# Batch 0's q side head by head, with its k-by-v sum turned by VectorE, and a new issue order batch by batch

## The chip, the cores and the metric

The kernel runs on one core of a Trainium2 chip. The metric is the device time of one execution in microseconds (us). TensorE is PE, VectorE DVE, ScalarE ACT, GpSimd POOL, and SyncE SP, which issues the transfers.

## The reference

```python
def phi(x):                       # x: [4 batches, 4 heads, 1088, 32]
    a = einsum('rd,bhsd->bhsr', S1, x); b = einsum('rd,bhsd->bhsr', S2, x)   # r = 8
    return einsum('bhsi,bhsj->bhsij', a, b).reshape(*x.shape[:-1], 64)
q_p, k_p = phi(q), phi(k)
kv = einsum('bhsf,bhsd->bhfd', k_p, v);  z = sum(k_p, axis=2)
attn = einsum('bhsf,bhfd->bhsd', q_p, kv) / (einsum('bhsf,bhf->bhs', q_p, z)[..., None] + 1e-06)
x = attn.transpose(0, 2, 1, 3).reshape(4352, 128)
h = x @ w_in                      # 128 -> 2048
out = (h - tanh(h)) @ w_out       # 2048 -> 128
```

The inputs and the output are float32; the two large products run in bfloat16.

## The kernel before

The work has two parts. **Attention** makes `xT`, the 4352 normalised rows turned to 128 partitions (4 heads of 32) by 4352 columns, batch by batch, 1088 columns each. The **FFN** takes `xT` in ten column groups (`GCOLS`), of 256, 384, 448, six of 512, and 192 columns. For each group `ffn` runs 16 matmuls `h` (one for each 128 rows of the hidden layer), 16 tanh `th` on ACT, 16 matmuls `o` with `w_out`, and two more `o` with `wch` and `wcl`, the product w_in·w_out in two bfloat16 halves, which stand for the linear part h @ w_out. The sum lies in PSUM bank 3; VectorE transposes it (`ot`) and SP stores it (`st`). The `h` results use PSUM banks 0 to 2, attention banks 4 to 7.

For each batch the **k side** transposes k (`kT`, VectorE), multiplies it by the small S1/S2 matrix (`ksk`, PE), transposes back (`kab`, VectorE), forms the 64 products of each row (`w`, three pieces of 768 columns, VectorE or POOL) and sums them with v (`kvmm`, three pieces of 24 matmuls on PE). `gram`, `gm`, `scmm` and `sc` get the weights of the denominator. `kv_tail` then turns the 128x64 sum into the stationary operand of the numerators: ACT or VectorE copies it out of PSUM four times side by side (`kvd`), PE transposes it (`kvt`), and it is copied out again (`kvb`).

The **q side** transposes q (`qT`), sketches it (`qsk`, PE, 16 tiles of 32x32, into four banks), transposes back (`abc`), makes the denominator and divides (`m`, `den`, `rd`, `aq`), forms the products (`qp`, pieces of 512 or 768 columns), transposes them (`qpT`) and multiplies by kv (`num`, PE, 32 matmuls of all 16 tiles, four banks). Two copies (`x`) put the result into `xT`. Batch 0's q side is cut into blocks 0 to 2 (256 columns) and 2 to 9, the latter with numerators for 2 to 5 and 5 to 9.

The names carry the batch and piece: `kT2.0.0` is batch 2's first k transpose, `h1.0` group 1's first matmul, `o1.3` its fourth of the second layer, `lk1.0` the first half of batch 1's k load. `wi` and `wo` are casts of the weights to bfloat16, `wit`/`wiT` a transpose of w_in on PE and its copy out by ACT, `wc` the product w_in·w_out on PE; all `wc` wait for the last `wo` cast.

Every engine issues its instructions in an order written out in `TABLE`: a token is an operation's number, the letter of its engine, and its buffer; `f` and `F` are filler matmuls on zeros, 256 and 512 columns long. `plan` reads it, and `sync` adds the waits. An engine that waits holds back all that is queued behind it. A load also waits until the loads ahead of it leave at most `CAP` bytes in flight:

```python
if o.big:
    left = CAP - o.dma[0]
    for p in reversed(loads):
        left -= p.dma[0]
        if left < 0:
            o.deps.setdefault(p, False)
```

The orders around the change, before:

```
PE   ksk0 6F gram0 f F scmm0 kvmm0.0 qsk0.0 kvmm0.1 F F wit0 wit1 kvmm0.2 wit2 kvt0 F F num0.0 wit3 qsk0.2 | h0.. o0.. wc.. num0.2 wc3 num0.5
     h1.0 h1.1 o0.11 ksk1 o0.12 h1.2 .. ksk2 .. kvmm1, gram1, kvmm2, kvmm3, kvt1-3 among h1, o1 | h2.. qsk1.0 qsk2.0 .. num1.0 h3.0-2 num1.5 .. qsk3.0 .. num2.0 in h4 .. num3.0 in h5
DVE  kT0 .. kab0.0 qT0.0 kab0.1 w0.0-2 abc0.0 den rd qpT0.0 qT0.1 abc0.2 m den rd qp0.2 qpT0.2 qpT0.5 qpT0.7 kT1.0.0 kT1.1.0 kT2.0.0 wcl kab1.0 kab1.1 x0.5.1 kT2.1.0 ot0 ..
ACT  gm0 sc0 wi0 wi1 wi2 kvd0 wo0 kvb0 wiT0 x0.0.0 x0.0.1 wiT1 th0.0 ..
POOL m0.0 aq0.0 qp0.0 wi3 wo1 wo2 wo3 aq0.2 qp0.5 qp0.7 w1.0 w1.1 w1.2 w2.0 w2.1 m1.0 qp1.. 
SP   lk0.0 sin1 lk0.1 lq0 lv0 lwi0-3 lwo0 lq0.1 lwo1-3 lk1 lq1 lv1 lk2 lq2 lv2 lk3.0 st0.0 lk3.1 lq3 ..
```

## Time and profile before

| | |
|---|---|
| Time, median of 3 runs | 112.78 us (111.4, 112.78, 112.95) |
| The profiled execution's own time | 111.28 us |
| Its span, first to last instruction | 109.1 us |
| Granted TensorE clock | 0.999 of full speed, the 2.4 GHz level |
| Busy PE / ACT / DVE / POOL | 97.9 / 80.8 / 58.4 / 30.3 us |
| HBM read / written | 8.95 / 2.23 MB |

Busy time of PE counts from the start of a matmul to its modelled end, and matmuls overlap, so a busy PE can still be waiting a little. A row of the timeline gives start, duration, engine, line, operation, output and input; in brackets stands the idle time ahead of it and what ended that. Lines of the code: L349 all copies, L438 loads, L528 `kT`, L540 `qT`, L548 `ksk`, L589 `w`, L604 `kvmm`, L622 `kvt`, L643 `qsk`, L686 `qp`, L702 `num`, L802 `h`, L806 `th`, L817 `o`, L826 `ot`.

### The profile page before, as it was taken

The numbers are of one execution on the slowest core, as the hardware profiler recorded it, in microseconds if no ns is written. First come the engines' busy times: TensorE is split into PE (matmuls) and PEld (weight loads), VectorE is DVE, ScalarE is ACT, GpSimd is POOL, SyncE is SP. The second block draws the span as 40 slices with busy tenths as digits, with TensorE's granted clock in tenths as the row PEclk, the third lists the DMA queues.
The fourth block names the chain that finished last, engine by engine and source line by source line (L and its number), as shares of the span: only waits on it lengthen the run. The fifth ranks groups of instructions, "written<-read, shape, count | busy, mean of one in ns | idle before, by whom it ended". The sixth has DMA issues, their size and how long they took to land.

```text
span 109.1 us, 3403 instructions
## 1 busy us (share of the span) xinstructions
PE 97.9 (90%) x1460; PEld 47.9 (44%) x1467; DVE 58.4 (54%) x91; ACT 80.8 (74%) x166; POOL 30.3 (28%) x48
## 2 busy tenths in 40 slices
...
GB/s 84 219 232 280 220 254 300 266 248 302 261 153 320 215 13 3 6 72 0 6 25 56 9 26 71 6 0 96 0 0 12 90 1 53 43 0 28 71 62 70
DMA packets 25918, 11.38 MB, mean 104 GB/s; under 512 B 19120, under 2 KB 23600, under 8 KB 25904
## 3 DMA queue, kind: packets, MB, share of 16 engines
...
q10 hardware_dynamic: 560, 0.07, 0.4%
...
HBM read 8.95 MB, written 2.23 MB: 102 GB/s over the span
## 4 chain that ended last, share of the span: by engine, by line
PE 54%; DMA 20%; DVE 10%; SPq 7%; POOL 3%; issue 2%
PE psb L817 22%; PE psb L802 20%; DMA wo_f<-in_moe_w_out_dram 8%; DMA kL<-in_k_dram 8%; SPq L438 7%; PE psb L702 5%; DMA wi_f<-in_moe_w_in_dram 5%; DVE kT L528 3%; PE psb L821 2%; POOL qp L686 2%; PE psb L604 2%; DVE w L589 2%; PE psb L643 1%; DVE abk L554 1%; DVE abc L648 1%
## 5 line engine op out<-in xcount | busy, mean ns | idle before, releaser
L806 ACT ACTIVATE th<-psb 128x512 bf16<-128x512 f32 (+4 forms) x136 | 70.1, 618 | 8.3 <-PE psb L802 5.8
L802 PE MATMUL psb<-xT,wi 128*128 128x512 bf16 (+4 forms) x154 | 46.3, 347 | 1.8 <-DVE wcl L788 1.0
L817 PE MATMUL psb<-th,wo 128*128 128x512 bf16 (+4 forms) x160 | 45.4, 348 | 0.4 <-issue 0.3
L802 PEld LDWEIGHTS psb<-xT,wi 128*128 128x128 bf16 x160 | 14.9, 97 | 23.8 <-ACT th L806 11.4
L826 DVE STREAM_TRANSPOSE ot<-psb 128x512 f32<-128x512 f32 (+4 forms) x10 | 6.3, 626 | 31.4 <-PE psb L817 31.4
L817 PEld LDWEIGHTS psb<-th,wo 128*128 128x128 bf16 x160 | 15.2, 98 | 13.2 <-issue 0.8
L686 POOL TENSOR_TENSOR qp<-ap,abc 128x512 f32<-128x512 f32 (+1 forms) x10 | 13.8, 1393 | 5.7 <-DVE ap L668 5.5
L691 DVE STREAM_TRANSPOSE qpT<-qp 128x768 f32<-128x768 f32 (+1 forms) x14 | 11.8, 854 | 2.8 <-POOL qp L686 2.6
L702 PE MATMUL psb<-qpT,kvb 32*32 32x128 f32 (+4 forms) x448 | 8.3, 309 | 1.7 <-ACT kvb L349 1.0
L528 DVE STREAM_TRANSPOSE kT<-kL 128x576 f32<-128x576 f32 (+3 forms) x10 | 5.9, 612 | 6.5 <-DMA kL<-in_k_dram 6.5
L589 POOL TENSOR_TENSOR w<-abk 128x768 f32<-128x768 f32 x5 | 7.5, 1518 | 5.6 <-DVE abk L554 5.6
L413 PE MATMUL psb<-zz 128*128 128x512 bf16 x21 | 7.5, 501 | 0.0
L702 PEld LDWEIGHTS psb<-qpT,kvb 32*32 32x32 f32 x448 | 5.2, 103 | 4.9 <-ACT kvb L349 1.5
L589 DVE TENSOR_TENSOR w<-abk 128x768 f32<-128x768 f32 x7 | 7.2, 1071 | 0.1
L648 DVE STREAM_TRANSPOSE abc<-psb 128x1152 f32<-128x1152 f32 (+2 forms) x5 | 5.7, 1140 | 1.8 <-PE psb L643 1.8
L660 POOL TENSOR_TENSOR m<-abc 128x288 f32<-128x288 f32 (+1 forms) x3 | 2.5, 844 | 14.4 <-DVE abc L648 14.4
L604 PE MATMUL psb<-w,vL 128*32 128x64 f32 x288 | 6.1, 222 | 0.3 <-POOL w L589 0.3
L540 DVE STREAM_TRANSPOSE qT<-qL 128x1088 f32<-128x1088 f32 (+2 forms) x5 | 5.2, 1057 | 0.9 <-DMA qL<-in_q_dram 0.9
L579 ACT COPY gm<-psb 128x32 f32<-128x32 f32 x4 | 0.8, 188 | 6.5 <-PE psb L569 6.5
L604 PEld LDWEIGHTS psb<-w,vL 128*32 128x32 f32 x288 | 4.6, 109 | 1.8 <-issue 0.6
L686 DVE TENSOR_TENSOR qp<-ap,abc 128x768 f32<-128x768 f32 x4 | 4.6, 1157 | 0.7 <-POOL ap L668 0.7
L548 PE MATMUL psb<-kT,wab 64*32 64x288 f32 x64 | 3.3, 472 | 1.7 <-DVE kT L528 0.9
...
## 6 DMA issues: line engine op xcount, KB each, us to landing
...
```

Of the source, the lines that this page charges most:

```text
L413: "F": lambda e, n: e.matmul(bank(3), zz.ap[:, 0:128], zz.ap[:, None, 128:384].to_broadcast([128, 2, 256]), start=True, stop=True)}, zop)
L438: op = P.add({x: 180.0 + 2.1 * rows for x in (eng if isinstance(eng, tuple) else (eng,))}, lambda e, n: e.dma_start(out=o_, in_=i_), w=w, ...
L528: P.add(_v(nb * 32 * (r1 - r0)), lambda e, n, e_=e_, nb=nb, r0=r0, r1=r1: e.transpose(kT[b].ap.rearrange("p (j u t r) -> p r j u t", u=2, ...
L589: P.add({**_v(768), **_gt(768)}, lambda e, n: e.tensor_tensor(out=wv.ap.rearrange("p (x i j) -> p x i j", i=8, j=8), in0=abh(0)[:, :, :, N ...
L604: i = e.matmul(pv[b].ap[h * 32:(h + 1) * 32, 0:64], vL[b][:, h, blk * 32:(blk + 1) * 32], wvs[b, p].ap[:, (bi * 4 + h) * 64:(bi * 4 + h + ...
L648: P.add(_vp(sn * 4), lambda e, n: e.transpose(abc.ap.rearrange("p k h f -> p h k f")[:, :, 0:s1 - s0, :], psa4[:, :, 0:sn].rearrange("p h ...
L686: P.add({**_v(cn * 256), **_gt(cn * 256)}, lambda e, n, qp=qp, c0=c0, cn=cn: e.tensor_tensor(out=qp.ap[:, 0:cn * 256].rearrange("p (x i j) ...
L691: P.add(_v(cn * 256), lambda e, n, qp=qp, o0=o0, cn=cn: e.transpose(qt.ap[:, o0 * 256:(o0 + cn) * 256], qp.ap[:, 0:cn * 256]), r=[qp], w=[ ...
L702: i = e.matmul(psa4[h * 32:(h + 1) * 32, g, 0:nb * 32], kvb.ap[g * 32:(g + 1) * 32, x, h * 32:(h + 1) * 32], qq[g * 32:(g + 1) * 32, 0:nb, ...
L802: P.add(_mm(n_), lambda e, n, jb=jb, hv=hv: e.matmul(hv.ap[:, jb % m * 512:jb % m * 512 + n_], wi[jb // 4].ap[:, (jb % 4) * 128:(jb % 4 + ...
L806: P.add(_a(n_ * m), lambda e, n, hv=hv, th=th: e.activation(out=th.ap.rearrange("p (u x) -> p u x", u=m)[:, :, 0:n_], in_=hv.ap.rearrange( ...
L817: fn = lambda e, n, x=x, st=st, sp_=sp_: e.matmul(ov.ap[:, 0:n_], wo[x // 4].ap[:, x % 4, :], ths[x][0].ap[:, ths[x][1] * 512:ths[x][1] * ...
```

## The change

- Batch 0's q side is cut at blocks of 8, 13 and 13 chunks of 32 columns (`CUT0`), so 256, 416 and 416 columns, and the first groups become 256, 416, 416. Each group of the first three now needs just one piece.
- `kv_heads` replaces `kv_tail(0)`: one VectorE transpose of the 128x64 sum (`kvh`), from PSUM to SBUF. `kvd0`, `kvt0` and `kvb0` go.
- `q_heads` sketches with 4 matmuls and makes numerators with 8, each on the tile of one head (rows and columns h·32), into one bank instead of four, and as long as the piece. Products come in pieces of 512; 448 and 384; 448 and 384 columns.
- Batch 0's remaining q load is cut as its two pieces are. `CAP` is 1.45e6 for 1.3e6. `occ` is a cost for the planner and does nothing on the chip.
- `TABLE` is new. Batch 1's k and q sides are issued ahead of batch 2's, and batch 3's k side moves from group 1 into groups 3 to 6.

```diff
--- before.py
+++ after.py
@@ -16,53 +16,54 @@
 AF = mybir.ActivationFunctionType
 AX = mybir.AxisListType
 
-GCOLS = [256, 384, 448] + [512] * 6 + [192]
-CAP = 1.3e6
+GCOLS = [256, 416, 416] + [512] * 6 + [192]
+CAP = 1.45e6
 PAIRS = 7
-PIECES = {0: [(0, 2), (2, 5), (5, 9)], 1: [(0, 5), (5, 9)], 2: [(0, 9)], 3: [(0, 9)]}
+CUT0 = [0, 8, 21, 34]
+PIECES = {1: [(0, 5), (5, 9)], 2: [(0, 9)], 3: [(0, 9)]}
 ENGINES = {"v": "vector", "a": "scalar", "g": "gpsimd", "t": "tensor", "s": "sync"}
 TABLE = """
...
 """
 
 
@@ -434,8 +435,8 @@
         P.add(_g(40), lambda e, n, b=b: e.memset(qpad[b].ap, 0.0), w=[qpad[b]], name=f"qpad{b}")
     vvals = [[_Val(ap=vL[b][:, h, :]) for h in range(H)] for b in range(B)]
 
-    def load(o_, i_, w, nbytes, rows, eng="sync", cap=True, name="", wait=()):
-        op = P.add({x: 180.0 + 2.1 * rows for x in (eng if isinstance(eng, tuple) else (eng,))}, lambda e, n: e.dma_start(out=o_, in_=i_), w=w, dma=(nbytes, nbytes / rows),
+    def load(o_, i_, w, nbytes, rows, eng="sync", cap=True, name="", wait=(), occ=415.0):
+        op = P.add({x: occ for x in (eng if isinstance(eng, tuple) else (eng,))}, lambda e, n: e.dma_start(out=o_, in_=i_), w=w, dma=(nbytes, nbytes / rows),
                    after=wait, name=name)
         op.big = cap
         return op
@@ -445,8 +446,8 @@
 
     kvals = [[_Val(ap=kL[b][:, r * 544:(r + 1) * 544]) for r in range(2)] for b in range(B - 1)]
     kvals.append(kvals[0])
-    qcut = {0: [0, 8, 34]}
-    qvals = [[(a, z, [_Val(ap=qL[b][:, a * 32:z * 32]) for _ in range(2 if z - a > 8 else 1)]) for a, z in zip(c[:-1], c[1:])]
+    qcut = {0: CUT0}
+    qvals = [[(a, z, [_Val(ap=qL[b][:, a * 32:z * 32]) for _ in range(2 if b else 1)]) for a, z in zip(c[:-1], c[1:])]
              for b, c in ((b, qcut.get(b, [0, 34])) for b in range(B))]
 
     def load_k(b):
@@ -460,12 +461,12 @@
         vs = v[b].rearrange("h (m x) d -> m h (x d)", x=17)
         for h in range(H):
             src = bass.AP(tensor=vs.tensor, offset=vs[:, h, :].offset, ap=[list(vs.ap[0]), [256, 2], [1, 288]])
-            load(vL[b][:, h, :], src, [vvals[b][h]], 128 * 1152, 128, name=f"lv{b}.{h}")
+            load(vL[b][:, h, :], src, [vvals[b][h]], 128 * 1152, 128, name=f"lv{b}.{h}", occ=615.0)
 
     def load_q(b, i):
         a, z, vals = qvals[b][i]
         src = q[b].rearrange("h (t c) d -> (h t) (c d)", c=NC)
-        cut = [a, z] if z - a < 9 else [a, (a + z) // 2, z]
+        cut = [a, (a + z) // 2, z] if b else [a, z]
         for j, (a0, z0) in enumerate(zip(cut[:-1], cut[1:])):
             load(qL[b][:, a0 * 32:z0 * 32], src[:, a0 * 32:z0 * 32], [vals[j]], 128 * (z0 - a0) * 128, 128, name=f"lq{b}.{i}.{j}")
 
@@ -487,6 +488,7 @@
         load_wi(i)
     load_wo(0)
     load_q(0, 1)
+    load_q(0, 2)
     for i in range(1, 4):
         load_wo(i)
     for b in range(1, B - 1):
@@ -625,6 +627,64 @@
         P.add({**_a(256), **_vp(256)}, lambda e, n: copy(
             e, n, kvb.ap.rearrange("p x c -> p (x c)"), pv[b].ap[:, 0:256]),
             r=[pv[b]], w=[kvb], name=f"kvb{b}")
+
+    kvh = _Val(ap=sb("kvh", [128, 64]))
+
+    def kv_heads():
+        P.add(_vp(64), lambda e, n: e.transpose(kvh.ap, pv[0].ap[:, 0:64]), r=[pv[0]], w=[kvh], name="kvh")
+
+    def q_heads(i):
+        c0, c1, (_, ) = qvals[0][i]
+        nx = c1 - c0
+        q_transpose(0, i)
+        qt_ = qTv[0][-1][2]
+        pq = _Val(first1 if i == 0 else att1)
+        abc, m_, dn, rd, aq = _Val(abc_p), _Val(m_p), _Val(den_p), _Val(rd_p), _Val(ap_p)
+
+        def sk(e, n):
+            for h in range(H):
+                r = e.matmul(pq.ap[h * 32:(h + 1) * 32, 0:nx * 32], wqs[0][h * 32:(h + 1) * 32, :],
+                             qt_.ap[h * 32:(h + 1) * 32, :], start=True, stop=True)
+            return r
+        P.add(_pe(90 + nx * 53.3, 230.0), sk, r=[qt_, scv[0], wqc[0]], w=[pq], mode="32x32", name=f"qsk0.{i}")
+        P.add(_vp(nx * 32), lambda e, n: e.transpose(
+            abc.ap.rearrange("p k h f -> p (k h f)")[:, 0:nx * 32], pq.ap[:, 0:nx * 32]), r=[pq], w=[abc], name=f"abc0.{i}")
+        pt = lambda x, a, z: abc.ap.rearrange("p k h f -> p (k h) f")[:, a:z, x * 8:(x + 1) * 8]
+        P.add({**_v(nx * 8), **_gt(nx * 8)}, lambda e, n: e.tensor_tensor(
+            out=m_.ap[:, 0:nx, 0:8], in0=pt(0, 0, nx), in1=pt(2, 0, nx), op=ALU.mult), r=[abc], w=[m_], name=f"m0.{i}", lock=True)
+        P.add(_v(nx * 9), lambda e, n: e.tensor_reduce(
+            out=dn.ap[:, 0:nx], in_=m_.ap[:, 0:nx, :], op=ALU.add, axis=AX.X), r=[m_], w=[dn], name=f"den0.{i}")
+        P.add(_vr(nx), lambda e, n: e.reciprocal(rd.ap[:, 0:nx], dn.ap[:, 0:nx]), r=[dn], w=[rd], name=f"rd0.{i}")
+        P.add({**_v(nx * 8), **_gt(nx * 8)}, lambda e, n: e.tensor_tensor(
+            out=aq.ap[:, 0:nx * 8].rearrange("p (x i) -> p x i", i=8), in0=pt(0, 0, nx),
+            in1=rd.ap[:, 0:nx, None].to_broadcast([128, nx, 8]), op=ALU.mult),
+            r=[abc, rd], w=[aq], name=f"aq0.{i}", lock=True)
+        qt = _Val(qpT_p)
+        cut = [0, nx] if nx < 9 else [0, (nx + 1) // 2, nx]
+        for a, z in zip(cut[:-1], cut[1:]):
+            qp = _Val(qp_p)
+            P.add({**_v((z - a) * 64), **_gt((z - a) * 64)}, lambda e, n, qp=qp, a=a, z=z: e.tensor_tensor(
+                out=qp.ap[:, 0:(z - a) * 64].rearrange("p (x i j) -> p x i j", i=8, j=8),
+                in0=aq.ap.rearrange("p (x i) -> p x i", i=8)[:, a:z, :, None].to_broadcast([128, z - a, 8, 8]),
+                in1=pt(1, a, z)[:, :, None, :].to_broadcast([128, z - a, 8, 8]),
+                op=ALU.mult), r=[abc, aq], w=[qp], name=f"qp0.{c0 + a}", lock=True)
+            P.add(_v((z - a) * 64), lambda e, n, qp=qp, a=a, z=z: e.transpose(
+                qt.ap[:, a * 64:z * 64], qp.ap[:, 0:(z - a) * 64]), r=[qp], w=[qt], name=f"qpT0.{c0 + a}")
+        pn = _Val(first1 if i == 0 else att1)
+
+        def num(e, n):
+            qq = qt.ap[:, 0:nx * 64].rearrange("p (c x t) -> p c x t", x=2, t=32)
+            for x in range(2):
+                for h in range(4):
+                    r = e.matmul(pn.ap[h * 32:(h + 1) * 32, 0:nx * 32], kvh.ap[h * 32:(h + 1) * 32, x * 32:(x + 1) * 32],
+                                 qq[h * 32:(h + 1) * 32, :, x, :], start=(x == 0), stop=(x == 1), skip_group_check=True)
+            return r
+        P.add(_pe(90 + nx * 106.7, 175.0), num, r=[kvh, qt], w=[pn], mode="32x32", name=f"num0.{i}")
+        for a, z in ((0, nx // 2), (nx // 2, nx)):
+            xv = _Val(ap=xT[:, (c0 + a) * 32:(c0 + z) * 32])
+            P.add({**_a((z - a) * 32), **_vp((z - a) * 32)}, lambda e, n, a=a, z=z, xv=xv: copy(
+                e, n, xv.ap, pn.ap[:, a * 32:z * 32]), r=[pn], w=[xv], name=f"x0.{i}.{int(a > 0)}")
+            xvals.append(((c0 + a) * 32, (c0 + z) * 32, xv))
 
     def q_in(b, s0, s1):
         return [v_ for (a, z, v_) in qTv[b] if a < s1 * 4 and z > s0 * 4]
@@ -729,22 +789,18 @@
 
     def attention():
         k_transposes(0)
-        q_transpose(0, 0)
         k_sketch(0)
         gram(0)
         for p in range(3):
             k_outer(0, p)
         kv_mm(0)
-        kv_tail(0)
-        st = q_front(0, 0, 2)
-        q_piece(0, 0, 0, 2, *st)
-        q_transpose(0, 1)
+        kv_heads()
+        q_heads(0)
         load_k(B - 1)
         load_q(B - 1, 0)
         load_v(B - 1)
-        st = q_front(0, 2, 9)
-        for b0, b1 in PIECES[0][1:]:
-            q_piece(0, 2, b0, b1, *st)
+        q_heads(1)
+        q_heads(2)
         for b in range(1, B):
             k_side(b)
             q_transpose(b, 0)
```

The orders around the change, after:

```
PE   ksk0 f 4F gram0 f F scmm0 F qsk0.0 f F wit0 kvmm0.0-2 wit1 wit2 wit3 f num0.0 qsk0.1 | h0.0-2 qsk0.2 h0.. o0.. wc0-3 h0.15 ksk1 num0.1 num0.2
     h1.0 o0.14 h1.1 o0.15 o0.16 h1.2 o0.17 h1.3 kvmm1.0 kvmm1.1 gram1 h1.4-6 ksk2 h1.7 h1.8 o1.0 kvmm1.2 scmm1 gram2 h1.9 h1.10 kvt1 scmm2 h1.11 h1.12 qsk1.0 .. |
     h2.. qsk2.0 .. h2.13 num1.0 o2.0 .. h3.0 .. h3.4 num1.5 .. ksk3 .. kvmm2 gram3 scmm3 kvt2 .. qsk3.0 h4.. num2.0 .. kvmm3.0 in h5, kvmm3.1-2 and kvt3 in h6, num3.0 before h6.14
DVE  kT0.0.0 mask4 mask2 kT0 .. wab qT0.0 kab0.0 kab0.1 w0.0-2 abc0.0 den rd qp0.0 kvh qpT0.0 qT0.1 qT0.2 abc0.1 m den rd abc0.2 qp0.8 den rd qpT0.8 aq0.2
     kT1.0.0 kT1.1.0 qpT0.15 qpT0.21 kab1.0 qpT0.28 kab1.1 qT1.0 wcl w1.1 kT2.0.0 kT2.1.0 ot0 kab2.0 kab2.1 qT2.0 kvb1 abc1.0 m1 den1 rd1 aq1 abc2.0 qpT1.0 qpT1.3 ot1 ..
ACT  gm0 sc0 wi0 wi1 wi2 wi3 wiT0 wiT1 x0.0.0 x0.0.1 th0.0 wo0 th0.1 .. th0.15 x0.1.0 x0.1.1 wch x0.2.0 th1.0 ..
POOL m0.0 aq0.0 wo1 aq0.1 m0.2 wo2 wo3 qp0.15 qp0.21 qp0.28 w1.0 w1.2 w2.0 w2.1 qp1.0 qp1.3 m2.0 qp1.5 qp1.7 w2.2 aq2.0 qp2.. m3.0 w3.0 aq3.0 qp3.0 w3.1 ..
SP   lk0.0 lk0.1 sin1 lq0 lv0 lwi0-3 lwo0 lq0.1 lq0.2 lwo1-3 lk1 lq1 lv1 lk2 lq2 lv2.0 st0.0 lv2.1-3 st0.1 lk3.0 ..
```

## Rows read from the trace of the kernel before

**Rows 1.** Windows, core 0: PE, PEld, DVE, ACT, POOL busy, clock, DMA.
```profile
17.62:53.36 35.74, 32.08 (x731) 17.57 (x724) 28.82 (x42) 23.47 (x64) 17.73 (x19) 1.00 0.54 157
...
53.36:106.02 52.66, 51.94 (x455) 23.86 (x460) 20.40 (x29) 50.26 (x89) 7.30 (x5) 1.00 0.21 33
```

**Rows 2.** Chain that ended last: start us, us, what.
```profile
71.32 0.43 PE psb L817 x2
...
72.83 1.53 PE psb L702 x63
...
106.02 0.38 DVE ot L826
```

**Rows 3.** Timeline, 10.8 to 18 us, up to the first group's matmuls.
```profile
10.83 1.97 ACT L349 CAST wi<-wi_f 128x512 bf16<-128x512 f32 x3 [0.84 <-DMA wi_f<-in_moe_w_in_dram]
...
13.09 0.37 ACT L349 COPY kvd<-psb 128x256 f32<-128x256 f32 x1 [0.30 <-PE psb L604]
...
13.52 0.44 PE L622 MATMUL psb<-ident,kvd 128*128 128x128 f32 x2 [0.16 <-ACT kvd L349]
...
14.96 0.36 ACT L349 COPY kvb<-psb 128x256 f32<-128x256 f32 x1
...
15.38 0.85 PE L702 MATMUL psb<-qpT,kvb 32*32 32x64 f32 x64 [0.99 <-ACT kvb L349]
...
15.82 1.04 DVE L540 STREAM_TRANSPOSE qT<-qL 128x832 f32<-128x832 f32 x1 [0.85 <-DMA qL<-in_q_dram]
...
16.60 1.02 ACT L349 COPY wiT<-psb 128x1024 bf16<-128x1024 bf16 x1
...
17.02 0.67 PE L643 MATMUL psb<-qT,wq 32*32 32x224 f32 x32 [0.46 <-DVE qT L540]
...
17.62 0.50 PE L802 MATMUL psb<-xT,wi 128*128 128x256 bf16 x3
...
17.94 2.32 ACT L806 ACTIVATE th<-psb 128x256 bf16<-128x256 f32 x8 [0.32 <-PE psb L802]
```

**Rows 4.** Waits of SP's queue: us in total, times, longest.
```profile
SPq L438 <- DMA wi_f<-in_moe_w_in_dram: 3.2, 1, 3.2
```

**Rows 5.** Timeline, VectorE: the smallest transpose and products alone.
```profile
5.75 0.20 DVE L497 STREAM_TRANSPOSE stt<-sin 128x64 f32<-128x64 f32 x1
...
8.75 2.69 DVE L589 TENSOR_TENSOR w<-abk 128x768 f32<-128x768 f32 x3
```

**Rows 6.** Timeline, 23 to 26 us: batch 0's later numerators.
```profile
23.01 0.96 PE L702 MATMUL psb<-qpT,kvb 32*32 32x96 f32 x64
...
24.79 1.06 PE L702 MATMUL psb<-qpT,kvb 32*32 32x128 f32 x64 [0.48 <-DVE qpT L691]
```

**Rows 7.** Timeline, 25 to 37 us: group 1 and the k sides.
```profile
25.78 0.50 PE L802 MATMUL psb<-xT,wi 128*128 128x384 bf16 x2
...
26.31 0.83 PE L548 MATMUL psb<-kT,wab 64*32 64x288 f32 x16
...
27.68 0.78 DVE L528 STREAM_TRANSPOSE kT<-kL 128x576 f32<-128x576 f32 x1 [1.79 <-DMA kL<-in_k_dram]
...
28.70 0.34 PE L802 MATMUL psb<-xT,wi 128*128 128x384 bf16 x1 [0.96 <-DVE wcl L788]
...
35.97 1.78 DVE L589 TENSOR_TENSOR w<-abk 128x768 f32<-128x768 f32 x1
```

**Rows 8.** Timeline, 40 to 54 us: values by k, and group 3's start.
```profile
40.36 0.88 PE L604 MATMUL psb<-w,vL 128*32 128x64 f32 x48
...
53.36 0.59 PE L802 MATMUL psb<-xT,wi 128*128 128x512 bf16 x2 [0.22 <-issue]
```

**Rows 9.** Groups by line and form, POOL.
```profile
L686 POOL TENSOR_TENSOR qp<-ap,abc 128x512 f32<-128x512 f32 x6 | 7.1, 1194 | 0.1
```

**Rows 10.** One line's DMA issues, 15.3 to 17 us, SP: durations ns, landing.
```profile
L438 SPq DMA_DIRECT2D kL<-in_k_dram x2: 341/362/382, 15.0 to 16.6; - x2
...
DMA to landing us min/median/max: 4.1/4.5/5.0
```

82 lines of the change are left out of this document (41 added, 41 removed).

## The prediction

> **What bounds the kernel now.** I read the windows first. The reader is to cut the span in two where group 3 starts, at 53.36 us. Behind it PE is busy 51.94 of 52.66 us [rows 1]. Ahead of it, from the first FFN matmul at 17.62 us, it is busy 32.08 of 35.74 us, and no other engine is full either [rows 1]. Next comes the chain: in the second part it is PE alone, at 0.43 us for two 512-column matmuls [rows 2]. So an FFN group of 512 columns costs 34 x 0.215 = 7.31 us, and the 4352 columns cost 62.1 us. The attention work on PE behind 17.62 us is three k sides (`ksk` 0.83, `kvmm` 1.32 from 0.88 for two, `kvt` 0.44, `gram` and `scmm` estimated at 0.4 together: 3.0 each [rows 3, 7, 8]), three `qsk` at some 0.7, `num1` 2.2, `num2` and `num3` 1.6 each, batch 0's last two `num` 2.02 [rows 6], and `wc`, estimated at 0.9. That makes 81.5 us of work in the 88.4 us from 17.62 to the last `ot` at 106.02 [rows 2]: PE waits 6.9 us. By the same sum the part behind 53.36 holds 51.5 us of work in 52.66, so 5.7 us of the waiting lie ahead of it. PE is the bound behind 53.36; ahead of it the order of queues is.
>
> The timeline then shows why. Up to 17.62 the path is the turn of kv: `kvd` at 13.09, `kvt`, and `kvb` only at 14.96, so that `num0.0`, which waited for it, runs at 15.38; then `qsk0.2` at 17.02, which waited for a q transpose that itself waited for its load [rows 3]. After 25.78, when group 1 starts, one case shows the manner: VectorE stands at batch 2's k transpose until its load lands at 27.68, `wcl` is queued behind it, and PE's next group 1 matmul starts at 28.70, released by `wcl` [rows 7]. All three k sides sit in group 1, so group 3 waits until 53.36 for batch 1's q side [rows 8].
>
> **The start of the FFN.** ACT no longer does `kvd0`, `kvb0` and, ahead of the first tanh, `wo0`; it takes `wi3` from POOL and does both `wiT` before the copies of `x0.0`. Its path: first load landed 10.83, four casts at 1.97/3 = 0.66 end at 13.46, two `wiT` at 1.02 end at 15.50, two copies estimated at 0.2 (under the 0.36 of a 256-column copy) at 15.9 [rows 3]. The other path is `qsk0.1`, which stands in front of `h0.0` on PE. It needs only the first half of the q load, where before the transpose waited for both halves until 15.82, VectorE having stood free for 0.85 us [rows 3]. So the first half's transpose starts between 14.97 and 15.82; it takes half of 1.04; `qsk0.1` has no row at 416 columns and is estimated at 0.75, above the 0.67 of 224 columns on sixteen tiles. `h0.0` then starts between 16.3 and 17.1. I take 16.3: SP stood 3.2 us for a w_in load [rows 4], and the larger `CAP` lets the load behind it go before that, which brings all later loads forward, by 0 to 2 us. `kvh` is a 64-column transpose, 0.20 at the nearest row, 0.44 at most by the matmul transposes of `kvt`; with `qp0.0` on VectorE at 512/768 of 0.90 = 0.60 [rows 5] it ends before 14.2 and hides behind ACT. If that cover were gone, it would cost its 0.2. The start moves by -1.3 us (ends -0.5 and -1.7).
>
> **PE's work.** From 96 to 128 columns a numerator's cost grows by 0.10 us per 32, 3.1 ns a column [rows 6]; 416 columns cost 1.30 and a fixed part. That is 0.66 with 32 matmuls and, for 8, taken as a quarter: 1.47 each (1.30 to 1.96). Two replace 2.02: +0.9 (0.6 to 1.9). `qsk0.2` now stands behind the start: +0.75 (0.5 to 1.0). The missing `kvt0` and the shorter list of fillers lie ahead of the start, where PE waits anyway: nothing. Together +1.7.
>
> Beside this stands a rule against the change. The Trainium skill, "TensorEngine Tiling (Array Packing)", section Theoretical Speedup, gives up to sixteen times where both small dimensions are 32 or less, and the new form fills only the four tiles on the diagonal. By it a column of `xT` costs four times as much array time as in the old form; the rows' slope gives less, since the old form pays 0.66 of 0.96 us as a fixed part. No row here shows four tiles alone.
>
> **The order.** I follow the queues with these durations, scaled by columns. ACT runs group 0's tanh at 2.32/8 = 0.29 each and `wo0` at 0.62: from 16.6 to about 21.9. VectorE goes without a rest from `abc0.1` through two `abc`, the small divisions, `qp0.8`, `qpT0.8` and `kT1`, which it reaches at 20.6; the k load of batch 1 was issued at 15.0 and 16.6 and landed at 20.0 and 20.7 [rows 10], so `kT1` does not wait, and ends at 22.1. PE does `ksk1` (0.83), `num0.1` and `num0.2` (1.47 each): `h1.0` at 26.0, against 25.78 before [rows 7]. POOL's three products at about 1.0 (1.194 for 512 columns [rows 9]) end at 23.3, one transpose ahead of `num0.2`. So the 1.3 us is given back here, in PE work put in front of group 1.
>
> From `h1.0` to `h3.0` PE then has 55 matmuls of 416 columns (0.175 each), four of 256, the rest of k side 1 (2.2), `ksk2`, `gram2`, `scmm2` (1.2), two `qsk` (1.5) and `num1.0` (1.2): 16.2 us. `wcl` now stands ahead of `kT2` on VectorE, and `kT2`'s wait falls on `ot0` and `w1.2`'s followers only; `num1.0` finds its transposes about 0.1 us early, POOL's `qp1.3` at 39.2 being the latest. With 0.5 us idle `h3.0` starts at 42.7, where before it started at 53.36 [rows 8]. More work is left then: 46.6 for groups 3 to 9, 13 matmuls `o2` (2.3), `num1.5` (1.1), k side 3 (3.0), `kvmm2` and `kvt2` (1.8), `qsk3` (0.7), `num2` and `num3` (3.2): 58.7 us. With the 1.1 us idle of before the end would be 102.5. I add 0.7 for waits that such a walk does not see: 103.2, 2.8 us earlier than 106.02. PE then waits 103.2 - 16.3 - 83.2 = 3.7 us in place of 6.9.
>
> The stores: `st0.0` now stands on SP ahead of `lv2.1` to `lv2.3`, and `st0`, `st1` and `st2` between batch 3's loads, so these wait for `ot0` to `ot2`. The first `kvmm` that needs them is in group 3 for batch 2 and in group 5 for batch 3: nothing, and at most the load's 4 to 5 us if `ot0` came after 40.
>
> One bound stays on VectorE. Three products of 768 took 2.69 us alone, 0.90 each, and one took 1.78 beside POOL's [rows 5, 7]. `qp0.8` and `w1.1` may meet POOL's products now: 0 to 1.4 us on VectorE's queue. I take 0.2 of it, inside the 0.7, since POOL casts `wo` while `qp0.8` runs. The Trainium skill, "GPSIMD Engine Reference", section 8, states that POOL shares its SBUF interfaces with VectorE instructions of two SBUF inputs. These two rows agree with that; by it both products would take double, which is the 1.4.
>
> **The rivals.**
> 1. *The waiting only moves.* At `h1.0` the new kernel is 0.2 us later, with `ksk1` and three matmuls `o0` (1.15 us) already done: 0.9 ahead. If the 5.7 us of waiting stay, in VectorE's full queue from 16 to 32 us, where each late product or load delays everything, the own time is 111.28 - 0.9 = 110.4. For it: VectorE has no rest there, and the POOL price above. Against it: the case of `wcl` is gone for certain.
> 2. *The diagonal tiles do not run side by side.* If a matmul on another row and column group waits for its neighbour, 1088 columns of numerators at 3.1 ns and of sketches at half that cost up to four times as much: 5.1 us becomes 20, 15 more. At two at a time it is 5.1 more: 111.28 - 2.8 + 5.1 = 113.6, slower. It decides from a factor of 1.55 on, where the 2.8 us is eaten. Against it: the old form's slope, the same for all sixteen tiles as 3.1 ns for one stream, shows tiles of different row and column groups at work together; only the order is new.
> 3. *The order is as tight as the work.* Waits of 1.5 us in all, loads 1 us earlier: end at 101.0, own time 106.3.
>
> That it would not do what it says is no separate case: `kvmm0` now stands behind `wit0`, so kv is no earlier, about 13.0 as before; only what follows is shorter.
>
> **How the numbers follow.** The profiled execution took 111.28 us, 2.18 more than its span, and lies 1.3% under the median of 112.78; the three runs go from 111.4 to 112.95. The forecast against it is 111.28 - 2.8 = 108.5, against the median in proportion 109.9; I take the middle, 109.2, since nothing tells which of these levels the next runs take. A measurement here tells about 2%, so faster means below 110.5 and slower above 115.0. Forecast 0.50 (107.2 to 110.5); rival 1 0.27 (110.0 to 112.6, nearly all within 2%); rival 2 0.07 (113.5 to 125); rival 3 0.10 (106.2 to 107.2); slower for a cause that I do not name 0.06, half of it within 2%. Faster: 0.47 + 0.10 = 0.57; slower 0.10; the rest 0.33. The range 106.2 to 112.4 leaves out rival 2, the unnamed cases and the last of rival 1, under 0.2.
>
> **What will show it.** Right: `h0.0` near 16.3, `h1.0` near 26, `h3.0` near 43, PE's busy share above 0.95 between them, `num0.1` at some 1.5 us, no wait for `wcl`. Wrong: `num0.1` over 2 us (rival 2); VectorE idle at `kT1` with PE waiting for `qpT0.28`, or `num1.0` waiting for `qpT1.3` (rival 1); `h0.0` at 17 or later would take 0.7 us off at once.

## The result, and the profile after

The changed kernel takes 105.5 us in the median (105.38 to 106.21, four runs), the kernel before 112.4 (111.4 to 112.95, four runs): ratio 0.941, interval 0.932 to 0.949, faster. The forecast was 109.2, its range 106.2 to 112.4: the direction is right, the size too small, and the time lies just below the range, on the side of rival 3 (106.3). The profiled execution took 105.42 us, 1.82 more than its span. Some executions of one and the same kernel are slower, and the ratios here are formed without them, so a ratio can differ from the quotient of two medians.

The windows come first again, cut at `h0.0`, `h1.0`, `h3.0` and the last `ot`. First the kernel before, where [rows 1] has the third window already (columns: window, its length, busy time and instructions of PE, PEld, DVE, ACT, POOL, granted clock, DMA share, GB/s):

```profile
17.62:25.78 8.16, 7.36 (x181) 4.50 (x172) 6.79 (x10) 5.50 (x18) 4.74 (x7) 1.00 0.88 279
25.78:53.36 27.58, 24.72 (x555) 13.07 (x553) 22.03 (x33) 17.98 (x46) 12.99 (x12) 1.00 0.44 120
```

And the changed kernel at the same four points:

```profile
15.42:25.07 9.65, 9.65 (x106) 4.41 (x103) 8.81 (x20) 6.03 (x20) 7.00 (x11) 1.00 0.90 293
25.07:41.66 16.59, 16.54 (x334) 8.70 (x332) 13.57 (x21) 15.70 (x41) 11.70 (x16) 1.00 0.49 132
...
41.66:100.52 58.86, 57.81 (x657) 28.45 (x663) 19.71 (x30) 52.92 (x95) 15.04 (x14) 1.00 0.25 42
```

From `h0.0` to the last `ot` PE was not busy for 0.80 + 2.86 + 0.72 = 4.38 us before and is not for 0.00 + 0.05 + 1.05 = 1.10 us now. With the start 2.20 us earlier, that is the 5.5 us by which the last `ot` is earlier (106.02 to 100.52), since the busy sum is the same 84.0. That it is the same surprises: by their own lines, numerators and sketches take 1.9 us more than before in this stretch (11.7 against 9.9). The busy time counts overlapping matmuls once, and a short wait between two of them counts as busy. Counted from the start of each matmul to the start of the next, waits included, the trace shows where the time went: the FFN's matmuls take 64.2 us in place of 68.0, numerators and sketches 11.7 in place of 9.9, all other matmuls 9.2 in place of 10.6. Together that is 85.1 in place of 88.4. So the FFN and the other attention matmuls, which wait less, more than make up for the dearer numerators and sketches.

The timeline of the changed kernel answers to [rows 3, 6, 7] (start, duration, engine, line, operation, output and input, count; in brackets the idle time ahead and what ended it):

```profile
7.65 2.70 DVE L591 TENSOR_TENSOR w<-abk 128x768 f32<-128x768 f32 x3
...
10.19 2.67 ACT L350 CAST wi<-wi_f 128x512 bf16<-128x512 f32 x4 [1.29 <-DMA wi_f<-in_moe_w_in_dram]
...
12.62 0.24 DVE L634 STREAM_TRANSPOSE kvh<-psb 128x64 f32<-128x64 f32 x1
...
12.77 1.93 ACT L350 COPY wiT<-psb 128x1024 bf16<-128x1024 bf16 x2
12.79 0.67 DVE L671 STREAM_TRANSPOSE qpT<-qp 128x512 f32<-128x512 f32 x1
...
13.52 1.06 PE L679 MATMUL psb<-qpT,kvh 32*32 32x256 f32 x16
...
14.59 0.90 PE L646 MATMUL psb<-qT,wq 32*32 32x416 f32 x8
14.65 0.56 ACT L350 CAST xT<-psb 128x128 bf16<-128x128 f32 x2
15.42 0.50 PE L858 MATMUL psb<-xT,wi 128*128 128x256 bf16 x3
...
22.14 3.00 PE L679 MATMUL psb<-qpT,kvh 32*32 32x416 f32 x32
25.07 0.35 PE L858 MATMUL psb<-xT,wi 128*128 128x416 bf16 x1
...
25.96 1.36 DVE L530 STREAM_TRANSPOSE kT<-kL 128x576 f32<-128x576 f32 x2
```

Three things are to be seen. `kvh` is one transpose of 0.24 us where `kvd`, `kvt` and `kvb` took from 13.09 to 15.32. `num0.0` ends at 14.58 and the second copy of the turned W_in at 14.70, so VectorE's path and ScalarE's arrive level at the copies of `x0.0`. PE arrives with them: `qsk0.1` follows `num0.0` at once and lasts until 15.49, when `h0.0` (15.42) has just begun. And batch 2's `kT` at 25.96 no longer waits for its load (before, 1.79 us [rows 7]). The two numerators of 416 columns take 3.00 together, 1.50 each. (The trace has two rows for each of these float32 matmuls, so x16 stands for 8 of them and x64 for 32.)

The chain of the changed kernel (start, duration, what), followed back from the first sketch at the top to the last `ot`, answers to [rows 2]. Up to `num0.0` it is mostly VectorE's work with few gaps, then PE's own:

```profile
5.83 0.92 PE psb L550 x16
...
7.65 2.70 DVE w L591 x3
10.35 0.37 DVE abc L650
...
12.87 0.60 DVE qpT L671
...
13.52 1.06 PE psb L679 x16
...
14.59 0.90 PE psb L646 x8
...
74.36 0.43 PE psb L873 x2
...
100.52 0.38 DVE ot L882
```

### The profile page after: what moved, and what is told of

Read it like the earlier page. It is cut to its first block, busy times and chain, and to the rows that moved or that the text cites. A ratio compares the mean times of both kernels' runs of the same rounds, so it can differ in the third digit from the quotient of the medians.

```text
span 103.6 us, 3035 instructions
## 1 busy us (share of the span) xinstructions
PE 96.9 (93%) x1272; PEld 47.0 (45%) x1280; DVE 52.1 (50%) x92; ACT 81.1 (78%) x166; POOL 36.2 (35%) x54
## 4 chain that ended last, share of the span: by engine, by line
PE 77%; DVE 10%; ACT 4%; DMA 3%; issue 2%; POOL 1%; DVEq 0%
PE psb L858 28%; PE psb L873 27%; PE psb L679 4%; PE psb L606 4%; ACT th L862 3%; PE psb L877 3%; PE psb L550 3%; DMA kL<-in_k_dram 3%; PE psb L762 3%; DVE w L591 3%; PE psb L703 2%; PE psb L646 2%; DVE kT L530 2%; DVE abc L708 1%; PE psb L837 1%
## 5 line engine op out<-in xcount | busy, mean ns | idle before, releaser
L858 PE MATMUL psb<-xT,wi 128*128 128x512 bf16 (+3 forms) x154 | 47.3, 348 | 0.9 <-issue 0.5
L873 PE MATMUL psb<-th,wo 128*128 128x512 bf16 (+3 forms) x159 | 44.5, 347 | 0.2 <-DVE ot L882 0.2
L882 DVE STREAM_TRANSPOSE ot<-psb 128x512 f32<-128x512 f32 (+3 forms) x10 | 6.3, 626 | 31.8 <-PE psb L873 31.8
L746 POOL TENSOR_TENSOR qp<-ap,abc 128x768 f32<-128x768 f32 (+1 forms) x10 | 13.6, 1378 | 3.0 <-DVE ap L728 2.9
L591 POOL TENSOR_TENSOR w<-abk 128x768 f32<-128x768 f32 x7 | 10.6, 1513 | 3.5 <-DVE abk L556 3.5
L751 DVE STREAM_TRANSPOSE qpT<-qp 128x768 f32<-128x768 f32 (+1 forms) x10 | 8.7, 880 | 3.4 <-POOL qp L746 3.3
L350 ACT CAST xT<-psb 128x128 bf16<-128x128 f32 (+5 forms) x10 | 3.6, 368 | 4.2 <-PE psb L679 2.5
L708 DVE STREAM_TRANSPOSE abc<-psb 128x1152 f32<-128x1152 f32 x3 | 4.1, 1382 | 2.6 <-PE psb L703 2.6
L762 PE MATMUL psb<-qpT,kvb 32*32 32x288 f32 (+2 forms) x256 | 5.5, 352 | 0.0
L556 DVE STREAM_TRANSPOSE abk<-psb 128x288 f32<-128x288 f32 x8 | 3.5, 462 | 2.5 <-PE psb L550 2.5
L679 PE MATMUL psb<-qpT,kvh 32*32 32x416 f32 (+1 forms) x48 | 4.1, 467 | 0.1
```

Of the source, the lines that this page charges most:

```text
L591: P.add({**_v(768), **_gt(768)}, lambda e, n: e.tensor_tensor(out=wv.ap.rearrange("p (x i j) -> p x i j", i=8, j=8), in0=abh(0)[:, :, :, N ...
L679: r = e.matmul(pn.ap[h * 32:(h + 1) * 32, 0:nx * 32], kvh.ap[h * 32:(h + 1) * 32, x * 32:(x + 1) * 32], qq[h * 32:(h + 1) * 32, :, x, :], ...
L746: P.add({**_v(cn * 256), **_gt(cn * 256)}, lambda e, n, qp=qp, c0=c0, cn=cn: e.tensor_tensor(out=qp.ap[:, 0:cn * 256].rearrange("p (x i j) ...
L751: P.add(_v(cn * 256), lambda e, n, qp=qp, o0=o0, cn=cn: e.transpose(qt.ap[:, o0 * 256:(o0 + cn) * 256], qp.ap[:, 0:cn * 256]), r=[qp], w=[ ...
L762: i = e.matmul(psa4[h * 32:(h + 1) * 32, g, 0:nb * 32], kvb.ap[g * 32:(g + 1) * 32, x, h * 32:(h + 1) * 32], qq[g * 32:(g + 1) * 32, 0:nb, ...
L858: P.add(_mm(n_), lambda e, n, jb=jb, hv=hv: e.matmul(hv.ap[:, jb % m * 512:jb % m * 512 + n_], wi[jb // 4].ap[:, (jb % 4) * 128:(jb % 4 + ...
```

## The experiments

The questions were: does the gain come from the order, from the new form of batch 0's q side, or only from both (1, 2, 5); what made the start earlier than forecast (3, 4, 6, 7); which part of the order took the waits away (8); and can the start be drawn in further (9 to 12). Ratios are to the kernel before, run on the same chip. The changed kernel itself was run again only beside 10 and 11, as 9 (105.52 us); the other experiments are set against its first time, 105.5.

**1. The new order with the old form.**

```diff
  CAP 1.45e6, TABLE in the new order
- PE  num0.0 qsk0.1 | h0.0-2 qsk0.2 .. h0.15 ksk1 num0.1 num0.2 h1.0   (8-matmul form, kvh)
+ PE  kvt0 num0.0 | h0.0-2 qsk0.2 .. h0.15 num0.2 ksk1 num0.5 h1.0     (32-matmul form, kvd/kvt/kvb)
```

> The new order and the new CAP, but batch 0's q side in its old form (kvd, kvt and kvb, both copies on VectorE; sixteen-tile sketches and numerators; pieces and groups of 256, 384, 448). Theory A, the order carries the gain behind the start: the FFN starts within 0.6 us of 15.4, PE has about 1.7 us less work behind it, group 3 starts near 41, and the time is 104.5 to 106.0 us. Theory B, the head-by-head form carries it (one bank for a piece in place of four, a short turn of kv): group 3 starts at 44 or later and the time is 107.5 to 109 us.

Measured: 111.74 us (110.47 to 113.45), ratio 1.004, interval 0.999 to 1.009. Two lines of its waits on the timeline, then its windows between `h0.0`, `h1.0` and `h3.0`:

```profile
15.39 0.40 PE L702 MATMUL psb<-qpT,kvb 32*32 32x64 f32 x29 [0.79 <-issue]
...
28.84 1.30 PE L702 MATMUL psb<-qpT,kvb 32*32 32x128 f32 x64 [1.60 <-DVE qpT L691]
```

```profile
16.43:30.07 13.64, 11.05 (x222) 6.21 (x223) 9.42 (x15) 6.61 (x20) 6.95 (x13) 0.75 0.71 213
30.07:47.80 17.73, 17.73 (x335) 9.10 (x330) 14.85 (x22) 15.92 (x41) 11.24 (x12) 0.92 0.40 104
```

Behind `h1.0` the order does here what it does in the changed kernel: no wait, 17.73 us to `h3.0` at a lower clock, against 16.59. But `h0.0` to `h1.0` takes 13.64 us against 9.65. So the order's gain is there, and is spent ahead of `h1.0`. My placement had a part in it: `qpT0.7` stood behind the `kab1` of VectorE. PE's clock is also lower up to 30 us (0.75 in the mean; this profiled execution, 112.36 us, lies 0.6 above the median). But the clock isn't what eats the gain: the one execution with a granted clock of 1.000 still took 110.47 us. So a better placement had to be tried (5).

**2. The old order with the new form.**

```diff
  kv_heads, q_heads, CAP 1.45e6 kept; TABLE in the order of before
+ PE  .. num0.0 wit3 qsk0.1 qsk0.2 h0.0 .. h0.15 num0.1 wc3 num0.2 h1.0 ..  (all k sides in group 1)
+ SP  lk0.0 sin1 lk0.1 ..
```

> The old order from the first instruction on, with the new CAP and batch 0's q side head by head (each old step replaced by its one or two new ones in the same place). Theory A, the order carries the gain: the three k sides are back in group 1, group 3 starts at 51 to 54 us and the time is 109.5 to 112 us. Theory B, the form carries it: group 3 starts near 45 us and the time is 106 to 108 us.

Measured: 112.70 us (111.94 to 113.15), ratio 1.018, interval 1.009 to 1.027. `h0.0` started at 18.40, behind both sketches, which my placement put ahead of it. Its window from `h1.0` to `h3.0`:

```profile
27.28:54.04 26.76, 24.76 (x555) 13.32 (x552) 22.42 (x32) 17.82 (x46) 12.93 (x11) 1.00 0.40 107
```

It looks like the window 25.78:53.36 of before: 2.00 us not busy against 2.86. In this placement the form alone gains nothing. Even with the start of the changed kernel, 3.0 us earlier, it would be at 109.7 by estimate.

**3. The old CAP.**

```diff
-CAP = 1.45e6
+CAP = 1.3e6
```

> The changed kernel with CAP at 1.3e6 again. If the larger CAP brought the first q piece early (it landed 1.05 us earlier than I took it), its load is issued only when the first w_in load has landed, qT0.1 starts 0.4 to 1.0 us later, the FFN starts at 15.8 to 16.4 and the time is 0.4 to 1.0 us over the changed kernel's. Rival, the earlier k load and transposes set the start: the FFN starts within 0.2 us of 15.42 and the time is within 0.3 us.

Measured: 106.24 us (105.67 to 106.58), ratio 0.959, interval 0.952 to 0.966. The VectorE timeline shows which load the larger CAP brings forward:

```profile
13.96 0.61 DVE L542 STREAM_TRANSPOSE qT<-qL 128x416 f32<-128x416 f32 x1 [0.58 <-DMA qL<-in_q_dram]
15.98 0.61 DVE L542 STREAM_TRANSPOSE qT<-qL 128x416 f32<-128x416 f32 x1 [1.41 <-DMA qL<-in_q_dram]
```

`h0.0` stays at 15.46. The last piece of batch 0's q comes late, `qsk0.2` waits 0.69 us for it, and `h1.0` is 1.1 us later. CAP is worth 0.7 us, behind the start.

**4. The whole head in its old order.**

```diff
- SP  lk0.0 lk0.1 sin1 ..
+ SP  lk0.0 sin1 lk0.1 ..
- DVE kT0.0.0 mask4 mask2 kT0.0.1 stt kT0.1.0 kT0.1.1 wab qT0.0 kab0.0 kab0.1 ..
+ DVE kT0.0.0 mask4 kT0.0.1 kT0.1.0 stt mask2 kT0.1.1 wab kab0.0 qT0.0 kab0.1 ..
```

> The changed kernel with the old order of the head alone: the S2 load between the halves of the first k load, mask2 behind stt, qT0.0 between the two kab0. If VectorE's chain from the k load to the first numerator sets the start, ksk0 goes back to about 6.6, the products of k to 8.75, the FFN starts 0.8 to 1.1 us later (16.2 to 16.5) and the time is 0.8 to 1.1 us over the changed kernel's. Rival, the landing of the weights and of the q piece sets it: 0 to 0.3 us.

Measured: 106.82 us (106.66 to 106.86), ratio 0.965, interval 0.962 to 0.969. The products start at 9.15 (changed kernel 7.65), W_in's cast at 11.17 (10.19), `h0.0` at 16.78 (15.42). The order at the head, which I had priced at nothing, is worth 1.3 us. VectorE's and PE's timelines:

```profile
14.89 1.06 DVE L543 STREAM_TRANSPOSE qT<-qL 128x416 f32<-128x416 f32 x2
...
15.03 1.06 PE L680 MATMUL psb<-qpT,kvh 32*32 32x256 f32 x16 [0.69 <-DVE qpT L672]
15.91 0.88 PE L647 MATMUL psb<-qT,wq 32*32 32x416 f32 x8
16.78 0.50 PE L859 MATMUL psb<-xT,wi 128*128 128x256 bf16 x3
```

**5. The old form, better placed in the new order.**

```diff
  against experiment 1:
- PE  f num0.0 .. h0.15 num0.2 ksk1 num0.5 h1.0 o0.14 h1.1 o0.15 o0.16 h1.2 ..
+ PE  f F F num0.0 .. h0.15 num0.2 h1.0 o0.14 h1.1 num0.5 o0.15 o0.16 h1.2 ksk1 ..
+ DVE x0.2.1 and x0.5.1 from ACT, qpT0.5 qpT0.7 ahead of kab1.0, kvd0 and kvb0 on DVE
```

> The changed kernel with batch 0's q side in its old form (two halves, four-head score tiles, 64-matmul numerators), but its three numerators put at other places of the new order than in the first experiment: the second half's scores no longer hold back batch 1's k side, its copies lie on VectorE, and each numerator has W_in matmuls ahead of it. If the order is what gained and the form only has to fit it: h0.0 at 15.4 to 15.8, h1.0 by 25.7, 105.5 to 107 us. If the small numerators themselves are needed (the banks that the old form's accumulators hold, the pause inside a 64-matmul tile, the lower granted clock that followed in the first experiment): h1.0 after 28, 109 us or more.

Measured: 114.18 us (113.22 to 115.62), ratio 1.020, interval 1.008 to 1.032. `h0.0` 16.48, `h1.0` 26.61, `h3.0` 50.23. PE's waits on the timeline, then three windows:

```profile
15.43 0.40 PE L702 MATMUL psb<-qpT,kvb 32*32 32x64 f32 x31 [0.76 <-issue]
...
22.09 0.28 PE L817 MATMUL psb<-th,wo 128*128 128x256 bf16 x1 [0.77 <-POOL wo L349]
...
28.18 1.07 PE L702 MATMUL psb<-qpT,kvb 32*32 32x128 f32 x64 [0.98 <-DVE qpT L691]
...
33.14 1.68 PE L604 MATMUL psb<-w,vL 128*32 128x64 f32 x48 [2.22 <-POOL w L589]
```

```profile
14.00:18.00 4.00, 2.58 (x100) 1.05 (x99) 1.18 (x2) 1.87 (x7) 0.61 (x1) 0.79 1.03 305
...
24.00:29.00 5.00, 3.48 (x148) 2.52 (x145) 2.98 (x6) 2.08 (x6) 1.77 (x5) 1.00 0.50 172
29.00:36.00 7.00, 4.66 (x114) 2.28 (x90) 5.22 (x8) 1.76 (x5) 3.84 (x3) 0.81 0.01 2
```

The waiting comes back in this placement too. The old form's second half is one chain: a turn of 896 columns, mask, sums, quotients and products of 768, so the second numerator runs at 25.10 and the third at 28.18; in the changed kernel both are done by 25.14. What is put ahead of that chain on VectorE delays the numerators (1); what is put behind it is batch 1's k side, and `kvmm1` waits 2.22 us for its products on POOL. Neither place that I tried has room for it in the new order. My expectation for the order theory (105.5 to 107) was wrong by more than 7 us. Two of its waits also have to do with POOL's `wo` casts, so this is one of the possible placements, not a proof for all.

**6. Only the load of S2 back between the k halves.**

```diff
- SP  lk0.0 lk0.1 sin1 ..
+ SP  lk0.0 sin1 lk0.1 ..
```

> The changed kernel with one DMA issue moved: the load of S2 goes back between batch 0's two k halves on SP. If the time at which the first part of W_in lands sets the start (the cast of it began at 10.19 in the changed kernel, 10.83 before): that cast at 10.9 to 11.6, h0.0 later by 0.5 to 1.0, 105.9 to 106.6 us. If the landing doesn't hang on that load, or something else sets the start: no milestone moves by over 0.2, 105.4 to 105.8.

Measured: 106.14 us (106.07 to 106.39), ratio 0.951, interval 0.942 to 0.960; 0.62 over the control (9). VectorE's and PE's timelines:

```profile
5.18 0.48 DVE L531 STREAM_TRANSPOSE kT<-kL 128x288 f32<-128x288 f32 x1 [0.72 <-DMA kL<-in_k_dram]
...
8.39 2.70 DVE L592 TENSOR_TENSOR w<-abk 128x768 f32<-128x768 f32 x3
...
14.26 1.07 PE L680 MATMUL psb<-qpT,kvh 32*32 32x256 f32 x16 [0.29 <-DVE qpT L672]
...
16.01 0.50 PE L859 MATMUL psb<-xT,wi 128*128 128x256 bf16 x3
```

VectorE waits 0.72 us for the second k half, and its products, the numerator and `h0.0` are later by 0.74, 0.74 and 0.59 (against the control of 9, 0.59, 0.59 and 0.54). W_in's cast is later too (10.72), but VectorE's chain, with `num0.0` until 15.33, ends last, 0.1 us behind ScalarE's. My expectation had named W_in's landing as the link; the size is right and the link is k's landing.

**7. Only VectorE's head back in its old order.**

```diff
- DVE kT0.0.0 mask4 mask2 kT0.0.1 stt kT0.1.0 kT0.1.1 wab qT0.0 kab0.0 kab0.1 ..
+ DVE kT0.0.0 mask4 kT0.0.1 kT0.1.0 stt mask2 kT0.1.1 wab kab0.0 qT0.0 kab0.1 ..
```

> The changed kernel with only VectorE's head in its old order (the upper mask behind the product with S, the first two k head tiles before the mask, the first q head tile between the two score copies); the loads stay as they are. If VectorE's chain to the scores is the other half of the earlier start: ksk0 0.5 to 0.8 later (5.83 in the changed kernel), the products from 8.3 on, h0.0 later by 0.4 to 1.3 and the time with it, 105.9 to 106.8. If ScalarE and the W_in transposes cover it, as my forecast had it: h0.0 by at most 0.2 later, 105.4 to 105.7.

Measured: 106.22 us (106.03 to 106.24), ratio 0.951, interval 0.944 to 0.958. Products at 8.26, numerator 14.12, `h0.0` 15.87: later by 0.61, 0.60 and 0.45. The two halves give 0.59 + 0.45 = 1.04 of the 1.36 of experiment 4; the rest shows only when both are back.

**8. Batch 2's k side and batch 3's scores forward, as before.**

```diff
- PE  h2.. (no k work) .. h3.. ksk3 kvmm2.0-2 gram3 scmm3 kvt2 ..
+ PE  h1.15 ksk3 h2.0 kvmm2.0 h2.1 kvmm2.1 kvmm2.2 h2.2 gram3 kvt2 h2.3 scmm3 h2.4 .. h3..
+ SP  lk3 ahead of st0.0, lv2.1-3 and lv3 ahead of st0.1; kT3, w2, kab3 and their like with them
```

> The changed kernel with batch 2's k side (its products, numerators and turn) and batch 3's scores moved forward, in between the W_in matmuls of batch 2, as in the order of before; the loads they need go first again, and nothing is added or left out. The work ahead of h3.0 grows by what is moved (about 4 us: h1.0 to h3.0 16.6 to some 20.5). If the lateness of these parts in the new order is what took the waits of TensorE away: 1 us or more of waits on landed loads and on VectorE or GpSimd comes back in that stretch, and the time is 106.5 to 109. If the order has slack there and the work merely moves: the last ot within 0.4, 105.3 to 105.9.

Measured: 109.94 us (109.67 to 110.71), ratio 0.986, interval 0.977 to 0.995. Windows at the same four points, and the longest wait:

```profile
15.34:25.89 10.55, 9.73 (x106) 4.51 (x103) 9.44 (x21) 6.15 (x20) 6.92 (x11) 1.00 0.93 290
25.89:47.60 21.71, 19.96 (x449) 10.34 (x447) 16.57 (x27) 16.72 (x45) 11.26 (x14) 1.00 0.47 123
...
47.60:105.44 57.84, 56.21 (x541) 26.70 (x547) 17.15 (x24) 52.29 (x92) 13.97 (x13) 1.00 0.20 31
```

```profile
35.88 0.84 PE L551 MATMUL psb<-kT,wab 64*32 64x288 f32 x16 [1.69 <-DVE kT L531]
```

PE's time not busy goes from 1.10 to 0.82 + 1.75 + 1.63 = 4.20 us, nearly what it was before (4.38), with nothing added or left out: 1.69 of it at `ksk3`, whose transposes stand behind batch 1's turn on VectorE; 0.59 at `qsk0.2`, whose piece of q came late as in 3; and about 0.6 more at tanh behind `h3.0`. The forecast's 1 us or more came back threefold, and the time lies 0.9 above the expected range. The last `ot` comes 4.92 us later than in the changed kernel (105.44), of which the waits are 3.1 and busy time 1.9 (85.9 us against 84.0); this profiled execution lies 0.8 above the median. So the lateness of these parts accounts for some 2.5 of the 3.3 us of saved waiting, the late piece of q left aside.

**9. The changed kernel again,** unaltered, as the control of 10 and 11.

> The changed kernel itself, unaltered, as the measure for the two that run with it. 105.3 to 105.8 us; h0.0 at 15.4 to 15.5.

Measured: 105.52 us (105.25 to 105.71), ratio 0.948, interval 0.942 to 0.954; `h0.0` 15.47.

**10. One of the three first products on GpSimd.**

```diff
- DVE w0.0 w0.1 w0.2 ..        ACT .. wiT0 wiT1 x0.0 ..     PE  num0.0 qsk0.1 h0.0-2 qsk0.2
+ POOL w0.0  DVE w0.1 w0.2 ..  ACT .. wiT0 x0.0 wiT1 ..     PE  num0.0 h0.0-2 qsk0.1 qsk0.2
```

> The changed kernel with the first of batch 0's three products w0 on GpSimd, the second copy of the turned W_in behind the cast of x0.0 on ScalarE, and the first three W_in matmuls ahead of qsk0.1. VectorE's chain carries 2.70 us of products in a row; if that chain sets the start, as the two half experiments on the head say, it is 0.4 shorter, the numerator starts near 13.15 and h0.0 near 15.05: 105.0 to 105.4. If a landing (W_in, the second piece of q) sets it by now, h0.0 moves by under 0.15 and the time stays at that of the control. If GpSimd's product holds up VectorE's two (both were slower side by side later in the kernel: 1.12 against 0.90): no gain or up to 0.3 lost.

Measured: 107.80 us (107.69 to 109.43), ratio 0.970, interval 0.963 to 0.977: 2.3 us lost. Its profiled execution is the slowest of the six, so I read the cause in 11. What 10 loses beyond 11 its trace shows all the same: `qsk0.1` stands behind the first three W_in matmuls, the second of which waits 0.52 us for the copy of W_in, so it runs only at 17.23 in place of 14.59, and VectorE is idle for 3.95 us until it turns those scores at 18.91 (changed kernel 15.56).

**11. The same, `qsk0.1` left ahead of the first group, q's pieces loaded before W_out's first part.**

```diff
  as 10, but PE  num0.0 qsk0.1 h0.0-2 qsk0.2
- SP  lwi0-3 lwo0 lq0.1 lq0.2 lwo1-3 ..
+ SP  lwi0-3 lq0.1 lq0.2 lwo0 lwo1-3 ..
```

> The same, but qsk0.1 stays ahead of the first W_in matmuls and the load of W_out's first part goes behind the two remaining pieces of batch 0's q, so that these land about 0.8 us earlier. If the landing of q is what is late next: h0.0 near 15.1 and h1.0 near 24.7, 104.9 to 105.3, at or below the run without it. If W_out's part is missed instead (its cast on ScalarE and the first W_out matmul come later): a wait for it on TensorE near 17 and nothing gained over the control.

Measured: 106.60 us (106.46 to 106.71), ratio 0.958, interval 0.953 to 0.963; 1.1 us lost. VectorE's, GpSimd's and PE's timelines, with VectorE's two products one by one (smallest, middle and largest duration in ns, first and last start):

```profile
7.75 3.15 DVE L592 TENSOR_TENSOR w<-abk 128x768 f32<-128x768 f32 x2
...
L592 DVE TENSOR_TENSOR w<-abk x2: 959/1615/2271, 7.7 to 8.6; 128x768 f32<-128x768 f32 x2
...
7.79 2.28 POOL L592 TENSOR_TENSOR w<-abk 128x768 f32<-128x768 f32 x1 [2.07 <-DVE abk L557]
...
16.73 0.39 PE L859 MATMUL psb<-xT,wi 128*128 128x256 bf16 x2 [0.63 <-ACT wiT L351]
```

VectorE alone did three products in 2.70 us; two of them beside POOL's one take 3.15. They don't share the time evenly: VectorE's first takes 0.96 us. POOL's, issued 0.04 later, takes 2.28 where 1.51 is what it takes alone. VectorE's second takes 2.27 and ends 0.82 after POOL's has ended at 10.07. So each waited for the one before it. The copy of W_in that I put behind `x0.0` holds a bank that the second W_in matmul needs: 0.63 us more. The third theory of 10's expectation is the right one, and dearer than it said. The Trainium skill, "SBUF — State Buffer", section SBUF: two separate sides, says that VectorE's instructions with two SBUF inputs and GpSimd's exclude each other for the whole instruction. This trace agrees, by these durations and by their sum: 0.90 x 2 and POOL's 1.51 alone (its `w` products later in the changed kernel) are 3.31 in a row, and 3.15 were measured.

**12. The first scores turned ahead of the third product.**

```diff
- DVE w0.0 w0.1 w0.2 abc0.0 den ..     SP  lwi0-3 lwo0 lq0.1 lq0.2 lwo1-3 ..
+ DVE w0.0 w0.1 abc0.0 w0.2 den ..     SP  lwi0-3 lq0.1 lq0.2 lwo0 lwo1-3 ..
```

> The changed kernel with two issues moved: the turn of the first q scores (abc0.0) goes ahead of the third product w0 on VectorE, so that GpSimd's mask step runs beside that product, and the load of W_out's first part goes behind the last two pieces of batch 0's q. All products stay on VectorE. If VectorE's chain sets the start: the numerator 0.2 to 0.3 earlier than 13.52, h0.0 15.1 to 15.3, 105.1 to 105.4 us. If the turn waits for the scores (they end near 9.6) and holds up the third product and with it the k side's numerators: h0.0 unchanged or up to 0.3 later, 105.4 to 105.9.

Measured: 105.70 us (105.53 to 107.24), ratio 0.950, interval 0.940 to 0.959; the control's has 0.948. Timeline of VectorE and GpSimd:

```profile
10.11 0.92 DVE L592 TENSOR_TENSOR w<-abk 128x768 f32<-128x768 f32 x1
...
10.27 0.94 POOL L654 TENSOR_TENSOR m<-abc 128x64 f32<-128x64 f32 x1 [4.57 <-DVE abc L651]
```

GpSimd's mask step, 0.32 us in the changed kernel, takes 0.94 beside VectorE's product and ends 0.2 after it. The sums start at 11.25 (11.14 in the changed kernel), the numerator at 13.62, `h0.0` at 15.42 as before: no gain. None of 10 to 12 beats the changed kernel.

## Why the prediction was right or wrong

**The failed step is the start.** The forecast took `h0.0` at 16.3, with -1.7 us as the far end; it came at 15.42, -2.2. The 16.3 is the path over `qsk0.1`: the turn of q's first half at 14.97 at the earliest, half of 1.04, then 0.75. But 14.97 is when VectorE came free in the kernel before, and the landing of W_in's first part at 10.83 is of that kernel too [rows 3]. In the changed kernel VectorE is free at 13.46. Its products start at 7.65 in place of 8.75 [rows 5], and from their end to the end of `qpT0.0` pass 3.1 us in place of 3.5. So q is turned from 13.92 on, and W_in's cast starts at 10.19. The new order moves the load of S2 behind the second k half and the mask and transposes on VectorE, both in the listing that I had, and the forecast put them at nothing. Put back one by one they cost 0.59 and 0.45 us of `h0.0`, together 1.36 (6, 7, 4).

With the old head `h0.0` starts at 16.78 (4), later than 16.3. There q is turned at 14.89, as forecast, but `qsk0.1` has to wait on PE for `num0.0`, which runs from 15.03 to 16.09. The forecast had no such wait. So there were two errors, 1.36 and some 0.5 us, of opposite sign, and that the start is off by only 0.9 is luck.

The sentence on `kvh` and VectorE, "it ends before 14.2 and hides behind ACT", stops too early as well: `qpT0.0` and `num0.0` follow, and the copies of `x0.0` need them. `kvh` ended at 12.86, but `num0.0` at 14.58, level with ScalarE's 14.70; in 6 and 7 VectorE's path ends last. That `CAP` would bring the first piece of q forward was wrong too: it is turned at 13.96 with the old `CAP` and at 13.92 with the new (3). The 0.7 us of `CAP` come at the last piece.

**The sum by terms.** The last `ot` came at 100.52, forecast 103.2. Of the 2.7 us, 0.9 are the start. From `h0.0` to `h1.0` the walk gave 9.7 and 9.65 were measured; from `h1.0` to `h3.0` 16.7 and 16.59. Behind `h3.0`, 58.7 us of work, 1.1 idle as before and "0.7 for waits that such a walk does not see" stood against 57.81 busy and 1.05 not busy: 1.6 too much, about half of it work, half waits. The forecast of waits, 3.7 us in place of 6.9, took all time from `h0.0` on less the priced work. By that count 85.1 - 83.2 = 1.9 are left now; by the windows it is 1.1 in place of 4.4. The 6.9 were too many: the windows gave only 3.66 + 0.72 = 4.38 [rows 1]. The walk itself, too, held 84.6 us of work and 2.3 of waits, and not 83.2 and 3.7. Rival 3, with waits of 1.5 and loads 1 us earlier, is nearest to what happened, and its 106.3 misses by 0.8.

**Two choices outside the mechanism** make up the rest of the 3.7 us: the own time around the span is 0.36 us shorter, and taking the middle between profiled execution and median added 0.7. The latter would have been right for a kernel that scatters as the one before does (110.2 to 113.9 over all its runs here); the changed kernel's ten runs lie within 105.25 and 106.21.

**What was right.** The two numerators of 416 columns: 1.47 each forecast, 1.50 measured, which refutes rival 2: from 256 to 416 columns a numerator grows from 1.06 to 1.50 us, 2.75 ns a column, no more than the 3.1 of the old form, so the four diagonal tiles do run side by side. `qsk0.2`: 0.75 forecast, 0.90 by the row of `qsk0.1`, its equal. PE's added work: 1.7 forecast, 1.9 by its own lines. The order: `h3.0` 11.7 us earlier than before, forecast 10.7, and no wait for `wcl` or for the k load. SP issued batch 1's first k load at 13.91 us, 1.1 earlier than before [rows 10]; the prediction had 0 to 2 for the loads. That is right in size alone: the forecast gave it to the larger `CAP`, and with the old one the load is issued at 13.95 (3). Rival 1, that the waiting only moves, is what happens with the new order and the old form (1, 5), not here.

**Order and form.** I had summed them as independent terms. They aren't: 111.7 and 114.2 with the order and the new `CAP` but the old form (ratios 1.004 and 1.020), 112.7 with the form and the new `CAP` but the old order (1.018), 105.5 with both. Of what the form does for the order, the runs show the finish of the numerators ahead of `h1.0`. They don't separate the shorter pieces from the one bank that an accumulator now takes in place of four; that stays open.
